# Chunks of 512 tokens in place of 384 in a fused linear-attention and feed-forward kernel

## The chip, the core and the metric

The kernel runs on one core of one Trainium2 chip. A core has five engines with queues of their own: TensorE (PE in the profile, its weight loads PEld), VectorE (DVE), ScalarE (ACT), GpSimd (POOL) and SyncE (SP), which here issues all DMAs. The metric is device time in microseconds, the median of three runs. TensorE reads operands from the on-chip SBUF and writes sums into eight PSUM banks of 128 partitions x 512 float32.

## The reference

```python
q, k, v: (8, 8, 576, 64) float32      # batch, heads, tokens, head width
kv  = einsum('bhsd,bhse->bhde', k, v)
out = einsum('bhsd,bhde->bhse', q, kv)
rms = sqrt(mean(out * out, axis=-1) + 1e-6)
x   = (out / rms * g_norm), heads side by side: (4608 tokens, 512)
h   = x @ w_in          # (512, 2048), float64 in memory
g   = h * cos(h)
y   = g @ w_out         # (2048, 512), float64 in memory -> (4608, 512)
```

## The kernel before

**Tiling.** The 4608 tokens are cut into twelve chunks of `CH = 384`, d_ff into sixteen tiles of 128. A *step* is one tile j of d_ff for one chunk. Its first half, `stage1_part`, forms h for 128 rows of d_ff and the chunk's tokens in one bank `ps_h`: four pairs of heads p, three products each (`w_hi x_hi`, `w_lo x_hi`, `w_hi x_lo`, for every factor is split into two float32r parts), so twelve matmuls of CH columns. Its second half, `stage2_part`, adds g times the tile of w_out into one bank `acc{t}` for each 128 tokens t of the chunk, three products of 512 columns each. There are 192 steps; the order of steps is chunk 0 with tiles 0 to 7, chunk 1 with tiles 0 to 7, chunk 0 with 8 to 15, chunk 1 with 8 to 15, and then each later chunk with all sixteen. The halves of chunks 0 and 1 go through DRAM (`part`).

**Between the halves** stands `act_part` (line 640): ki on ACT (the number of turns), r twice on DVE, a clip of r on DVE, the sine of r on ACT, `r = h * r` on DVE (the last reader of the bank), ghi on ACT and glo on DVE.

**Beside the steps.** `w_part` turns the float64 words of a weight tile into float32r parts: three operations m on DVE, two sg on ACT, a product sg on DVE or POOL, a copy on ACT and a difference (`wi<-sg`, `wo<-sg`) on DVE or POOL. All 32 weight tiles stay in SBUF. `kv_part` forms k^T v of a pair of heads, `x_part` a chunk's normalised x for one pair: a transpose, a split of q into qhi and qlo, products with kv, a square, a transpose and a sum on DVE, an exchange on ACT, the power on POOL, a transpose, a product, xhi on ACT and xlo. For chunks 0 and 1 ("front"), x uses TensorE's transposes. A later chunk's x is made beside the steps of the chunk before it.

**Order.** The generators above don't run on the chip: class `Order` simulates the engines with the durations written in the `yield "run"` lines and with tokens for the buffers, and instructions are issued in the order in which its engines start them. `Pinned` keeps that order, so each engine works through a fixed list, and an instruction that waits holds up all behind it. `due(i) = 20 + 4 i` is the time a step is planned for. The buffers that matter: three `ps_h` banks, three `acc` banks, two `ps_a` banks (kv and x); two ki, three r, three g; two whole chunks of xhi and xlo; pools of three for `m` and `sg` and two for qhi and qlo; two `ob` tiles for output. At the program's end the last output tile uses the slot of `kt` instead of `ob`.

All engine instructions that go through `Pinned` have line 190 in the profile, so groups are told apart by tile names.

Of the kernel before, what the change touches and what calls it, by code (L numbers as in the profile page):

```python
# [23 lines left out]
# 2*pi = C1 + C2; C1 has 8 significant bits, so k * C1 is exact for |k| < 2**16.  # L24
# [3 lines left out]
# The upper word of a float64, read as a float32, grows with the float64 as sign and magnitude.  # L28
# 2**-126, float32's smallest normal number, reads as 1.125 * 2**-15; this scale takes it just above 0.5.
# [20 lines left out]
class Order:  # L50
    """Puts the program's parts in an order by a simulation of the engines.

    A part of the program is a generator. It yields what it needs next: ("run", [(engine, us), ...], prio)
    for the use of one of these engines, ("wait", events) or ("take", tokens). After a "run" it issues its
    instructions, in the order in which the simulated engines start them; the lowest prio goes first.
    """
# [3 lines left out]
    def __init__(self):  # L60
        self.busy = {}
        self.pending = []
        self.seq = 0

    def spawn(self, gen, t=0.0):
        self.advance(Proc(gen, t), None)

    def advance(self, proc, value):
        while True:
            try:  # L70
                req = proc.gen.send(value)
            except StopIteration:
                return
# [55 lines left out]
            # the engine is taken by the lowest prio among the parts ready when it would start  # L129
# [10 lines left out]
def tile_kernel(  # L140
# [16 lines left out]
    CH = 384  # L157
# [5 lines left out]
    # The first chunks and batches are loaded in fewer transfers, and lean on TensorE, which waits then.  # L163
# [13 lines left out]
    ps_h = ctx.enter_context(tc.tile_pool(name="ps_h", bufs=3, space=bass.MemoryType.PSUM))  # L177
# [4 lines left out]
    class Pinned:  # L182
        """An engine whose instructions stay in the order in which they are issued."""
# [11 lines left out]
    def copiers(on_act, on_dve):  # L195
        return [("ACT", on_act, 0.0), ("DVE", on_dve, 0.3)]
# [18 lines left out]
    # products of zeros, for TensorE's clock is at its half until it has been busy for a while  # L215
# [28 lines left out]

    def due(i):
        return 20.0 + 4.0 * i
# [22 lines left out]
    x_slot = [Event() for _ in range(NCH)]  # L269
# [46 lines left out]
    def kv_loads_front(b, p, tags):  # L316
        """The loads of an early pair of heads, into slots of weights that come late."""
# [22 lines left out]
    def q_loads_front(c, p, tag):  # L340
        """A chunk of pairs p and p + 1, in rows of tokens."""
# [27 lines left out]
    def kv_part(b, p, prio):  # L369
        yield "wait", [kv_in[b, p]] + ([q_used[c, p] for c in chunks_of(b - 2)] if b > 1 else [])  # L370
        yield "take", t_psa, prio
        _, end = yield "run", [("PE", 0.95 if b >= FRONT else 1.1)], prio if b < FRONT else -1.0
# [14 lines left out]
        else:  # L387
            e, end = yield "run", copiers(0.21, 0.27), prio
# [6 lines left out]
        yield "run", [("ACT", 0.21)], prio  # L395
# [6 lines left out]
        _, end = yield "run", [("DVE", 0.27)], prio  # L402
# [9 lines left out]
    def kv_split_part(b, p, prio):  # L412
        """The parts of an early kv, for a chunk that isn't."""
        yield "wait", [kv_done[b, p]]
        yield "run", [("ACT", 0.18)], prio
# [8 lines left out]
    def x_tiles(c):  # L424
        yield "take", t_x
        _, _ = yield "run", [("NONE", 0.0)], -1.0
        xs[c] = (
            xpool.tile([P, NP, CH], F32R, name="xhi"),
            xpool.tile([P, NP, CH], F32R, name="xlo"),
        )  # L430
        sched.fire(x_slot[c], sched.busy["NONE"])
# [6 lines left out]
    def x_part(c, p, prio):  # L438
        yield "wait", [q_in[c, p], x_slot[c]]
        front = c < FRONT  # L440
        yield "take", t_qhl, prio
        if front:
            bank = t_psa if c else t_h
            yield "take", bank, prio
            _, _ = yield "run", [("PE", 0.4)], prio
# [6 lines left out]
        else:  # L452
            yield "take", t_qT
            _, end = yield "run", [("DVE", 0.47)], prio
# [3 lines left out]
        if front:  # L458
            e, end = yield "run", copiers(0.41, 0.47), prio
            qT = at.tile([P, CH], F32, name="qhi")  # L460
            copy(e, qT, ps_t[:, 0:CH])
            sched.give(bank, end)
        else:
            yield "run", [("ACT", 0.41)], prio
            qhi = at.tile([P, CH], F32R, name="qhi")
            qlo = at.tile([P, CH], F32R, name="qlo")
# [6 lines left out]
        bank = t_acc[p] if c == 0 and p < NTT else t_psa  # L473
        yield "take", bank, prio
        _, end = yield "run", [("PE", 0.5 if front else 0.5 if len(parts) == 1 else 0.7)], prio if front else -1.0
# [12 lines left out]
        sched.give(t_qhl, end)  # L488
        yield "take", t_s1, prio
        yield "run", [("ACT", 0.37)], prio  # L490
        sq = at.tile([P, CH], F32, name="s1", bufs=4)
        act.activation(out=sq, in_=ps[:, 0:CH], func=AF.Square, scale=0.125)
        if front:
            t_xn = t_r if c == 0 and p < NTT else t_s1
            yield "take", t_xn, prio
            _, end = yield "run", [("ACT", 0.46)], prio
            x = ew.tile([P, CH], F32, name="r") if t_xn is t_r else at.tile([P, CH], F32, name="s1", bufs=4)
            act.activation(out=x, in_=ps[:, 0:CH], func=AF.Copy, scale=gcol)
            _, end = yield "run", [("PE", 0.6)], prio
            sums = ps[:, CH:CH + 2 * NTT]  # L500
# [3 lines left out]
            yield "run", [("DVE", 0.13)], prio  # L504
            ms = small.tile([P, 2 * NTT], F32, name="ms")
            dve.tensor_scalar(out=ms, in0=sums, scalar1=EPS, scalar2=None, op0=ALU.add)
            yield "run", [("POOL", 1.2)], prio
            rinv = small.tile([P, 2 * NTT], F32, name="rinv")
            pool.tensor_tensor(out=rinv, in0=ms, in1=mhalf[:, 0:2 * NTT], op=ALU.pow)
            yield "run", [("ACT", 0.41)], prio  # L510
# [3 lines left out]
            _, end = yield "run", [("PE", 0.4)], prio  # L514
# [4 lines left out]
            _, end = yield "run", [("DVE", 0.47)], prio  # L519
            dve.tensor_tensor(out=x, in0=x, in1=ps[:, 0:CH], op=ALU.mult)  # L520
            sched.give(bank, end)
        else:
            t_xn = t_s1
            yield "take", t_s2
            yield "run", [("DVE", 0.47)], prio
            sqT = at.tile([P, TB, 32], F32, name="s2", bufs=1)
            dve.transpose(out=sqT.rearrange("p a b -> p (a b)"), in_=sq)
            _, end = yield "run", [("DVE", 0.47)], prio
# [3 lines left out]
            sched.give(t_s2, end)  # L532
            yield "run", [("ACT", 0.41)], prio
# [3 lines left out]
            yield "run", [("DVE", 0.09)], prio  # L537
            ms = small.tile([P, TB], F32, name="ms")
            dve.scalar_tensor_tensor(out=ms, in0=part, scalar=EPS, in1=swp, op0=ALU.add, op1=ALU.add)
            yield "run", [("POOL", 2.28)], prio  # L540
# [20 lines left out]
    def w_part(key, prio):  # L561
# [40 lines left out]
        sched.give(t_wst, end)  # L602
        sched.fire(w_done[key], end)

# [1 line left out]
    g_done = [Event() for _ in steps]  # L606
    g_tiles = {}

# [207 lines left out]
```

## Time and profile before

| what | us |
|---|---|
| runs: median (lowest to highest) | 937.34 (936.47 to 938.5) |
| profiled execution: span from first to last instruction (its only time given) | 933.4 |
| PE, DVE, ACT, POOL busy in it | 898.7, 722.4, 487.0, 221.2 |
| first-half matmuls, 128x384 | 2304 |
| second-half matmuls, 128x512 | 1728 |
| DMA of the whole run (not a time) | 58.59 MB |

PE's matmuls overlap one another: a matmul of 384 columns shows as 340 ns, though the next one starts earlier. The distance of starts, not the duration, says what a matmul costs. An engine that waits inside an instruction, as DVE does for a resource, shows as busy.

### The profile page before, as it was taken

What the parts mean: (1) busy time and instruction counts of PE and PEld (TensorE: products, weight loads), DVE (VectorE), ACT (ScalarE), POOL (GpSimd) and SP (SyncE); (2) the same over time, 40 slices, a digit from 0 to 9 for tenths busy, and PEclk for the clock granted to TensorE, in tenths of its full rate; (3) what the DMA queues carried; (4) which work ended last, traced back from release to release, by engine and by line L of the source; (5) the groups of instructions that cost most, each with busy time, mean ns of one, the idle gap of its engine ahead of it and who ended that gap; (6) DMA issues with size and microseconds to landing.
All of it is one profiled execution on the core that took longest, in us unless ns stands there. A gap on an engine that the chain in (4) does not pass through costs nothing.

```text
span 933.4 us, 14111 instructions
## 1 busy us (share of the span) xinstructions
PE 898.7 (96%) x5008; PEld 798.7 (86%) x5008; DVE 722.4 (77%) x1442; ACT 487.0 (52%) x1094; POOL 221.2 (24%) x148
## 2 busy tenths in 40 slices
PE   8797878999999999999999999999999999999998
PEld 6685666889889998888889999889889999999997
DVE  3999999799777777777776876786886886886664
ACT  5876666455445445455445545454553653653443
POOL 3676655122120220121120220210210220220000
PEclk7899999999999999999999999999999999999999
DMA  9997001153211102121220111220310110100000
GB/s 253 261 314 233 35 0 57 18 161 99 68 42 43 18 9 69 43 60 47 58 67 25 27 18 30 72 69 9 94 18 1 51 18 1 52 1 1 35 1 34
DMA packets 112246, 58.59 MB, mean 63 GB/s; under 512 B 80432, under 2 KB 103984, under 8 KB 112176
## 3 DMA queue, kind: packets, MB, share of 16 engines
q1 hardware_dynamic: 112176, 57.70, 22.9%
q8 instruction: 39, 0.64, 0.3%
q14 instruction: 31, 0.25, 0.1%
HBM read 46.66 MB, written 11.01 MB: 62 GB/s over the span
## 4 chain that ended last, share of the span: by engine, by line
PE 83%; DVE 10%; DMA 3%; issue 1%; SPq 1%; ACT 0%; DVEq 0%
PE acc L190 39%; PE ps_h L190 39%; PE ps_a L190 5%; DVE m L190 4%; DVE r L190 3%; DVE glo L190 2%; DMA wo<-in_moe_w_out_dram 2%; DMA wi<-in_moe_w_in_dram 1%; SPq L364 1%; DMA wo<-in_v_dram 1%; SPq L321 1%; DVE xlo L190 0%; DVE sg L190 0%; DVE s L190 0%; SPq L348 0%
## 5 line engine op out<-in xcount | busy, mean ns | idle before, releaser
L190 PE MATMUL ps_h<-xhi,wi 128*128 128x384 f32 x1536 | 398.2, 340 | 8.8 <-DVE r L190 7.7
L190 PE MATMUL acc<-wo,ghi 128*128 128x512 f32 x1152 | 363.4, 397 | 1.0 <-ACT ghi L190 0.7
L190 PEld LDWEIGHTS ps_h<-xhi,wi 128*128 128x128 f32 x1536 | 282.5, 190 | 26.3 <-DVE r L190 10.2
L190 PE MATMUL ps_h<-xlo,wi 128*128 128x384 f32 x768 | 259.8, 338 | 0.0
L190 PEld LDWEIGHTS acc<-wo,ghi 128*128 128x128 f32 x1152 | 212.2, 189 | 37.7 <-ACT ghi L190 1.6
L190 PE MATMUL acc<-wo,glo 128*128 128x512 f32 x576 | 229.6, 399 | 11.2 <-DVE glo L190 11.1
L190 POOL TENSOR_TENSOR rinv<-ms,mhalf 128x12 f32<-128x12 f32 (+1 forms) x48 | 105.4, 2197 | 443.3 <-DVE ms L190 296.0
L190 ACT ACTIVATE r<-r,half_pi 128x384 f32<-128x384 f32 x192 | 117.9, 615 | 144.4 <-DVE r L190 143.2
L190 DVE TENSOR_TENSOR glo<-r,ghi 128x384 fp32r<-128x384 f32 x192 | 116.6, 608 | 44.0 <-ACT ghi L190 38.6
L190 DVE SCALAR_TENSOR_TENSOR r<-ki,ps_h 128x384 f32<-128x384 int32 x192 | 104.9, 547 | 59.1 <-ACT ki L190 57.7
L190 PEld LDWEIGHTS ps_h<-xlo,wi 128*128 128x128 f32 x768 | 145.1, 189 | 0.0
L190 DVE TENSOR_TENSOR r<-ps_h,r 128x384 f32<-128x384 f32 x192 | 106.1, 553 | 50.2 <-ACT r L190 49.5
L190 PEld LDWEIGHTS acc<-wo,glo 128*128 128x128 f32 x576 | 108.6, 189 | 40.0 <-DVE glo L190 16.5
L190 ACT ACTIVATE ki<-ps_h 128x384 int32<-128x384 f32 x192 | 94.0, 490 | 93.1 <-PE ps_h L190 92.1
L190 ACT CAST ghi<-r 128x384 fp32r<-128x384 f32 x192 | 98.1, 512 | 76.6 <-DVE r L190 75.6
L190 DVE SCALAR_TENSOR_TENSOR r<-ki,r 128x384 f32<-128x384 int32 x192 | 121.0, 631 | 3.1
L190 DVE TENSOR_SCALAR r<-r 128x384 f32<-128x384 f32 x192 | 75.1, 392 | 3.8
L190 POOL TENSOR_TENSOR sg<-m,sg 128x512 f32<-128x512 f32 x28 | 38.7, 1383 | 38.6 <-DVE m L190 24.1
L190 ACT CAST xhi<-s 128x384 fp32r<-128x384 f32 x45 | 23.1, 513 | 47.1 <-DVE s L190 47.0
L190 POOL TENSOR_TENSOR qlo<-qT,qhi 128x384 fp32r<-128x384 f32 x18 | 20.3, 1125 | 93.4 <-ACT qhi L190 72.5
L190 ACT COPY swp<-part 32x12 f32<-32x12 f32 x160 | 31.8, 199 | 11.4 <-DVE part L190 9.2
L190 ACT ACTIVATE s<-ps_a 128x384 f32<-128x384 f32 x45 | 21.9, 486 | 14.8 <-PE ps_a L190 14.6
(104 smaller groups left out, 639.0 us busy)
## 6 DMA issues: line engine op xcount, KB each, us to landing
out_dram<-ob SPq DMA_DIRECT2D x35, 256.0 KB, 2.1
wi<-in_moe_w_in_dram SPq DMA_DIRECT2D x16, 512.0 KB, 8.4
wo<-in_moe_w_out_dram SPq DMA_DIRECT2D x16, 512.0 KB, 9.8
kt<-in_k_dram SPq DMA_DIRECT2D x24, 256.0 KB, 2.8
vt<-in_v_dram SPq DMA_DIRECT2D x24, 256.0 KB, 3.1
qb<-in_q_dram SPq DMA_DIRECT2D x112, 48.0 KB, 2.1
qb<-in_q_dram SPq DMA_DIRECT2D x96, 24.0 KB, 1.8
part<-ob SPq DMA_DIRECT2D x6, 256.0 KB, 2.1
```

The source lines that it names most:

```text
L190: return lambda *a, **kw: tc.keep_in_program_order(f(*a, **kw))
L321: nc.sync.dma_start(out=t, in_=src[b, 2 * p:2 * p + 2].rearrange("h (p i) d -> p h i d", p=SF))
L364: nc.sync.dma_start(out=t, in_=src)
```

## The change

The chunk becomes 512 tokens: nine chunks, 144 steps, twelve matmuls of 512 columns in a step's first half and four times three of 512 columns in the second. The fourth `acc` bank is taken from `ps_h`, which keeps two. Room in SBUF comes from sharing: xhi and xlo are single pairs now, six slots of each, so that four hold the current chunk and two the next (pairs 2 and 3 of chunk 0 lie in the slots of `kt` and `vt`, so the first later loads of k and v wait for chunk 0's last step); qhi and qlo use the slots `m` and `sg` of the weights, three in all (`t_two`); ki has one slot; the square's transpose shares the slot of qT, and `s1` has three slots. The planner's durations come from formulas (`dve_us`, `act_us`), a step is planned for 5.4 us, and kv of a batch is made in the window of the first chunk that needs it, no longer a chunk earlier. The two `ob` slots stay as they are. The diff without comments and plain renamings:

```diff
-    CH = 384
+    CH = 512
...
-    xpool = ctx.enter_context(tc.tile_pool(name="xpool", bufs=2))
-    wst = ctx.enter_context(tc.tile_pool(name="wst", bufs=3))
+    xpool = ctx.enter_context(tc.tile_pool(name="xpool", bufs=6))
...
-    at = ctx.enter_context(tc.tile_pool(name="at", bufs=2))
+    at = ctx.enter_context(tc.tile_pool(name="at", bufs=3))
...
-    ps_h = ctx.enter_context(tc.tile_pool(name="ps_h", bufs=3, space=bass.MemoryType.PSUM))
+    ps_h = ctx.enter_context(tc.tile_pool(name="ps_h", bufs=2, space=bass.MemoryType.PSUM))
...
+    def dve_us(f=CH, rate=1):
+        return 0.15 + f / (960 * rate)
+
+    def act_us(f=CH):
+        return 0.18 + f / 1200
...
-        return [("DVE", 0.067 + f / 960, bias), ("POOL", 0.15 + f / 480, 0.0)]
+        return [("DVE", dve_us(f), bias), ("POOL", 0.2 + f / 410, 0.0)]
...
+    STEP = 5.4
     def due(i):
-        return 20.0 + 4.0 * i
+        return 20.0 + STEP * i
...
-    t_kv, t_q, t_qT, t_qhl = Tokens(2), Tokens(2), Tokens(1), Tokens(2)
-    t_s1, t_s2, t_psa = Tokens(4), Tokens(1), Tokens(2)
-    t_x, t_wst, t_h, t_ki, t_r, t_g, t_osb = Tokens(2), Tokens(3), Tokens(3), Tokens(2), Tokens(3), Tokens(3), Tokens(2)
+    t_kv, t_q, t_qT, t_two = Tokens(2), Tokens(2), Tokens(1), Tokens(3)
+    t_s1, t_psa = Tokens(3), Tokens(2)
+    t_x, t_h, t_ki, t_r, t_g, t_osb = Tokens(6), Tokens(2), Tokens(1), Tokens(3), Tokens(3), Tokens(2)
...
+    def x_tokens(c, p):
+        return t_kv if c == 0 and p >= 2 else t_x
...
-        yield "run", [("ACT", 0.41)], prio
-        xhi, xlo = xs[c]
-        act.copy(out=xhi[:, p, :], in_=x)
-        e, end = yield "run", either(CH), prio
+        t_slot = x_tokens(c, p)
+        yield "take", t_slot, prio
+        yield "run", [("ACT", act_us())], prio if front else due(begin[c]) - 2 * STEP
+        if t_slot is t_kv:
+            xhi, xlo = (
+                kvp.tile([P, 2, SI, D], F32R, name=n).rearrange("p h i d -> p (h i d)") for n in ("kt", "vt"))
+        else:
+            xhi, xlo = (xpool.tile([P, CH], F32R, name=n) for n in ("xhi", "xlo"))
+        act.copy(out=xhi, in_=x)
+        e, end = yield "run", either(CH), prio if front else due(begin[c]) - 2 * STEP
...
-        ki = ew.tile([P, CH], I32, name="ki", bufs=2)
+        ki = ew.tile([P, CH], I32, name="ki", bufs=1)
...
-        first, n = window(chunks_of(b)[0] - 1)
+        first, n = window(chunks_of(b)[0])
         for p in range(NP):
-            i = first + 2 + p * (n - 3) // NP
-            load(2.1, due(i) - 6.0, [kv_in[b, p]], kv_loads(b, p), take=t_kv)
+            i = first + p * (n - 4) // NP
+            load(2.1, due(i) - 6.0, [kv_in[b, p]], kv_loads(b, p),
+                 wait=[x_done[0, 2], x_done[0, 3]], take=t_kv)
```

**Where the lists change, first place: PE in the middle of the program.** Before, at the end of a chunk: the second half of a step (tile 14, three accumulators) stands between two whole first halves, and each first half (eight rows, twelve matmuls) has its bank.

```order
L190 MATMUL ps_h_6922<-xhi_5434,wi15_1649 128x384 x2
L190 MATMUL ps_h_6922<-xlo_5435,wi15_1649 128x384
L190 MATMUL acc0_6281<-wo14_1684,ghi_6926 128x512 x2
L190 MATMUL acc0_6281<-wo14_1684,glo_6927 128x512
L190 MATMUL acc1_6299<-wo14_1684,ghi_6926 128x512 x2
L190 MATMUL acc1_6299<-wo14_1684,glo_6927 128x512
L190 MATMUL acc2_6306<-wo14_1684,ghi_6926 128x512 x2
L190 MATMUL acc2_6306<-wo14_1684,glo_6927 128x512
L190 MATMUL ps_h_6955<-xhi_6152,wi0_239 128x384 x2
```

With the change, in the middle of a chunk, a second half (tile 11, four accumulators) stands inside the first half of tile 13; the next row begins the first half of tile 14.

```order
L193 MATMUL ps_h_5897<-xhi_5105,wi13_1445 128x512 x2
L193 MATMUL ps_h_5897<-xlo_5106,wi13_1445 128x512
L193 MATMUL acc0_5281<-wo11_1483,ghi_5894 128x512 x2
L193 MATMUL acc0_5281<-wo11_1483,glo_5895 128x512
L193 MATMUL acc1_5292<-wo11_1483,ghi_5894 128x512 x2
L193 MATMUL acc1_5292<-wo11_1483,glo_5895 128x512
L193 MATMUL acc2_5310<-wo11_1483,ghi_5894 128x512 x2
L193 MATMUL acc2_5310<-wo11_1483,glo_5895 128x512
L193 MATMUL acc3_5316<-wo11_1483,ghi_5894 128x512 x2
L193 MATMUL acc3_5316<-wo11_1483,glo_5895 128x512
L193 MATMUL ps_h_5897<-xhi_5113,wi13_1445 128x512 x2
L193 MATMUL ps_h_5897<-xlo_5114,wi13_1445 128x512
```

What moved: the first half of tile 14 reuses the bank of tile 12, and between the two PE has only tile 13's first half and one second half.

**Second place: DVE while the weights are converted.** Names m are weights, r and glo the chain of `act_part`, ms and xlo early x. Before:

```order
L190 TENSOR_TENSOR glo_1198<-r_1118,ghi_1197 128x384
L190 TENSOR_SCALAR r_1192<-r_1192 128x384
L190 TENSOR_SCALAR m_1148<-m_1148 128x512
L190 TENSOR_SCALAR m_1228<-wi11_851 128x512
L190 SCALAR_TENSOR_TENSOR r_1231<-ki_1218,ps_h_1173 128x384
L190 TENSOR_TENSOR r_1192<-ps_h_1093,r_1192 128x384
L190 SCALAR_TENSOR_TENSOR r_1231<-ki_1218,r_1231 128x384
L190 SCALAR_TENSOR_TENSOR m_1228<-wi11_851,m_1228 128x512
L190 TENSOR_TENSOR glo_1255<-r_1192,ghi_1254 128x384
```

With the change, around the same weight tile:

```order
L193 TENSOR_TENSOR glo_1227<-r_1165,ghi_1226 128x512
L193 TENSOR_SCALAR r_1218<-r_1218 128x512
L193 TENSOR_SCALAR m_1254<-wi11_706 128x512
L193 SCALAR_TENSOR_TENSOR m_1254<-wi11_706,m_1254 128x512
L193 TENSOR_TENSOR r_1218<-ps_h_1149,r_1218 128x512
L193 SCALAR_TENSOR_TENSOR r_1277<-ki_1269,ps_h_1222 128x512
L193 TENSOR_SCALAR m_1286<-wo9_720 128x512
L193 TENSOR_TENSOR glo_1280<-r_1218,ghi_1279 128x512
```

What moved: little; from one glo to the next stand the same four operations of the chain and about three of the weights, the chain's now 512 wide.

**Third place: the end of ACT's list,** the copies of the last accumulators to output. Before:

```order
L190 ACTIVATE r_9673<-r_9673,half_pi_93 128x384
L190 CAST ghi_9694<-r_9673 128x384
L190 COPY ob_9710<-acc0_9212 128x512
L190 COPY ob_9716<-acc1_9219 128x512
L190 COPY kt_9718<-acc2_9225 128x512
```

With the change:

```order
L193 CAST ghi_8243<-r_8219 128x512
L193 COPY ob_8253<-acc0_7713 128x512
L193 COPY ob_8258<-acc1_7719 128x512
L193 COPY kt_8265<-acc3_7729 128x512
L193 COPY ob_8268<-acc2_7724 128x512
```

What moved: a fourth copy stands at the end, and its tile `ob` is one of the two that acc0 and acc1 went out through.

More of the change, by code (lines that the diff above doesn't have):

```diff
@@ L387, in kv_part @@
         else:
-            e, end = yield "run", copiers(0.21, 0.27), prio
+            e, end = yield "run", [("ACT", 0.41, 0.0), ("DVE", 0.45, 0.3)], prio
             for j in range(2):
@@ L531, in x_part @@
             sched.give(t_s1, end)
-            sched.give(t_s2, end)
-            yield "run", [("ACT", 0.41)], prio
+            sched.give(t_qT, end)
+            yield "run", [("ACT", 0.8)], prio
             swp = small.tile([P, TB], F32, name="swp")
@@ L601, in w_part @@
         w_split[key] = w
-        sched.give(t_wst, end)
+        sched.give(t_two, end)
         sched.fire(w_done[key], end)
@@ L628, in stage1_part @@
             w = w_split["wi", j]
-            xhi, xlo = xs[c]
+            xhi, xlo = xs[c, p]
             cols = slice(p * P, (p + 1) * P)
@@ L753, in tile_kernel @@
                 sched.spawn(g_part())
-    for c in range(NCH):
-        sched.spawn(x_tiles(c))
     for c in range(FRONT):
@@ L786, in tile_kernel @@
     sched.run()
+    assert not sched.live, sorted({x.gen.__name__ for x in sched.live})
 _INS = ['q', 'k', 'v', 'g_norm', 'moe_w_in', 'moe_w_out']
```

149 lines of the change are left out of this document (73 added, 76 removed).

## The prediction

> **What bounds the kernel now.** I read the page first: the busy shares, the slices over time, and the chain that ended last.
>
> ```profile
> span 933.4 us, 14111 instructions
> PE 898.7 (96%) x5008; PEld 798.7 (86%) x5008; DVE 722.4 (77%) x1442; ACT 487.0 (52%) x1094; POOL 221.2 (24%) x148
> PE   8797878999999999999999999999999999999998
> DVE  3999999799777777777776876786886886886664
> PE 83%; DVE 10%; DMA 3%; issue 1%; SPq 1%; ACT 0%; DVEq 0%
> ```
>
> The slices (23 us each) show two regimes: for seven slices DVE stands at 9 and PE at 7 or 8, after that PE never falls below 9. The chain, in order of time, says where one gives way to the other, and the busy times by stretch say how completely.
>
> ```profile
> 162.24 1.60 DVE glo L190
> 163.89 1.87 PE acc L190 x7
> 165.76 2.62 PE ps_h L190 x15
> ...
> 0.00:40.00 40.00, 32.65 (x280) 27.05 (x280) 23.43 (x44) 26.22 (x57) 20.85 (x27) 0.87 1.08 257
> 40.00:165.76 125.76, 102.05 (x499) 84.18 (x500) 124.22 (x193) 82.69 (x165) 79.56 (x57) 0.93 0.42 132
> 165.76:929.80 764.04, 764.04 (x4230) 687.49 (x4229) 574.75 (x1207) 377.48 (x872) 120.77 (x65) 1.00 0.16 40
> 929.80:933.40 3.60, 0.01 (x1) 0.00 (x0) 0.00 (x0) 0.58 (x1) 0.00 (x0) 1.00 0.57 219
> ```
>
> Columns after the length are PE, PEld, DVE, ACT and POOL busy. From 40 to 165.76 us DVE is busy 124.22 of 125.76 us and sets the pace (it converts the weights there); from 165.76 to 929.80 PE is busy without a gap at clock 1.00; 3.60 us of output follow. So the change is worth what it does to DVE's list before 165.76, to PE's list after it, and what new holes it tears in PE.
>
> **PE's list.** The main question is whether a matmul of 512 columns costs less per column than one of 384. Starts of runs in PE's timeline:
>
> ```profile
> 842.02 0.63 PE L190 MATMUL acc<-wo,ghi 128*128 128x512 f32 x2
> ...
> 844.10 0.51 PE L190 MATMUL ps_h<-xhi,wi 128*128 128x384 f32 x2
> ...
> 848.29 0.63 PE L190 MATMUL acc<-wo,ghi 128*128 128x512 f32 x2
> ```
>
> Nine 512-wide ones from 842.02 to 844.10 are 231.1 ns each, 0.4514 ns a column; 24 of 384 from 844.10 to 848.29 are 174.6 ns each, 0.4547 a column. Columns are the same in sum (192 x 12 x 384 = 144 x 12 x 512, and 1728 sums of 512 in both), so width by itself gives 884,736 x 0.0033 ns = 2.9 us and no more. What moves time is how much of PE's list is done while DVE is the bound:
>
> ```profile
> L190 PE MATMUL ps_h<-xhi,wi 128*128 128x384 f32 x173 | 49.4, 366 | 8.8 <-DVE r L190 7.7 <-POOL wi L190 1.0
> L190 PE MATMUL acc<-wo,ghi 128*128 128x512 f32 x120 | 40.3, 418 | 1.0 <-ACT ghi L190 0.7 <-ACT ob L190 0.2
> L190 PE MATMUL ps_h<-xlo,wi 128*128 128x384 f32 x86 | 30.0, 349 | 0.0
> L190 PE MATMUL acc<-wo,glo 128*128 128x512 f32 x60 | 26.0, 433 | 11.2 <-DVE glo L190 11.1
> ```
>
> These are PE's groups from 0 to 165.76: 259 / 12 = 21.6 first halves of steps and 180 / 9 = 20.0 second halves. Left over are 170.4 x 12 x 174.6 ns = 357.0 and 172 x 9 x 231.1 = 357.7, together 714.7 us; the other 49.3 of the 764.04 are kv and x. With 512, the same 21.6 and 20.0 steps carry a third more tokens, and left over are 122.4 x 12 x 231.1 = 339.5 and 124 x 12 x 231.1 = 343.9, together 683.4. **PE's term: -31.3.** kv has the same products; x has 43,008 columns times pairs and parts left instead of 46,080, 1.4 us, of which more narrow pieces take some: **-1**.
>
> **DVE's list up to there.** The thirty-two weights are the same work. Up to the twentieth glo, DVE's list holds 96 weight operations before and after, 100 of the element-wise chain in both, and in all 233 against 237 instructions (the extra ones small copies, against two products that move to POOL: about nothing). So the chain's operations are counted once per step, and grow. What 512 costs over 384:
>
> ```profile
> L190 DVE TENSOR_TENSOR r<-ps_h,r 128x384 f32<-128x384 f32 x192 | 106.1, 553 | 50.2 <-ACT r L190 49.5
> L190 DVE TENSOR_TENSOR ob<-ob,acc 128x512 f32<-128x512 f32 x6 | 4.0, 674 | 0.0
> ...
> 110.55 0.35 DVE L190 TENSOR_SCALAR r<-r 128x384 f32<-128x384 f32 x1
> 111.16 0.41 DVE L190 TENSOR_SCALAR m<-m 128x512 int32<-128x512 int32 x1
> ```
>
> +121 ns for an operation on tensors, +60 for the clip: 4 x 121 + 60 = 0.54 us a step, 10.9 for 20 steps, and 16 such operations in the early x (a product and an xlo for eight pairs) 1.9: **+13 is the lower end.** But many early durations are longer than that:
>
> ```profile
> 113.85 1.65 DVE L190 TENSOR_TENSOR glo<-r,ghi 128x384 fp32r<-128x384 f32 x1
> 117.13 0.54 DVE L190 SCALAR_TENSOR_TENSOR r<-ki,ps_h 128x384 f32<-128x384 int32 x1
> 118.57 0.55 DVE L190 SCALAR_TENSOR_TENSOR r<-ki,r 128x384 f32<-128x384 int32 x1
> ...
> 113.77 1.32 POOL L190 TENSOR_TENSOR sg<-m,sg 128x512 f32<-128x512 f32 x1 [0.45 <-DVE m L190]
> 116.61 1.75 POOL L190 TENSOR_TENSOR wo<-sg,wo 128x512 fp32r<-128x512 f32 x1
> ```
>
> glo begins 0.08 us after a POOL product and lasts 1.65 instead of 0.55, to 0.41 us after POOL's end; r<-ki,ps_h, which reads PSUM, runs in 0.54 beside POOL. If all durations grew by a third, waits included, the chain's five operations up to 180 us bound it:
>
> ```profile
> L190 DVE TENSOR_TENSOR glo<-r,ghi 128x384 fp32r<-128x384 f32 x23 | 22.1, 963 | 2.3 <-ACT ghi L190 2.3
> L190 DVE SCALAR_TENSOR_TENSOR r<-ki,r 128x384 f32<-128x384 int32 x24 | 20.7, 866 | 0.1
> L190 DVE TENSOR_TENSOR r<-ps_h,r 128x384 f32<-128x384 f32 x24 | 13.1, 548 | 2.6 <-ACT r L190 2.6
> L190 DVE SCALAR_TENSOR_TENSOR r<-ki,ps_h 128x384 f32<-128x384 int32 x24 | 12.9, 541 | 0.0
> L190 DVE TENSOR_SCALAR r<-r 128x384 f32<-128x384 f32 x24 | 10.2, 429 | 0.2
> ```
>
> The five means give 3.35 us a step, and 20 x 1.1 + 2 is **+24, the upper end.** I take **+16**, near the lower: the wait ends with POOL's instruction, which is a weight's and keeps its size. The Trainium skill, "SBUF — State Buffer", section "SBUF: two separate sides", says that DVE and GpSimd hold a shared pair of ports by an exclusive lock for a whole instruction; these rows agree, and by that rule alone the term would be +13, by growth in proportion +24.
>
> **Waits that the change makes.** ps_h has two banks instead of three. A bank is held from the first product of a step until `r = h * r` has read it. One such chain of before, ACT and DVE:
>
> ```profile
> 841.84 0.34 PE L190 MATMUL ps_h<-xlo,wi 128*128 128x384 f32 x1
> 842.28 0.49 ACT L190 ACTIVATE ki<-ps_h 128x384 int32<-128x384 f32 x1 [1.21 <-PE ps_h L190]
> 842.80 0.56 DVE L190 SCALAR_TENSOR_TENSOR r<-ki,ps_h 128x384 f32<-128x384 int32 x1 [1.14 <-ACT ki L190]
> 843.77 0.52 DVE L190 SCALAR_TENSOR_TENSOR r<-ki,r 128x384 f32<-128x384 int32 x1
> 844.73 0.35 DVE L190 TENSOR_SCALAR r<-r 128x384 f32<-128x384 f32 x1
> 845.27 0.62 ACT L190 ACTIVATE r<-r,half_pi 128x384 f32<-128x384 f32 x1
> 845.91 0.56 DVE L190 TENSOR_TENSOR r<-ps_h,r 128x384 f32<-128x384 f32 x1
> ```
>
> From PE's end (842.18) to the release (846.47) are 4.29 us, with three operations of x between. At 512 the six operations gain 3 x 0.12 + 0.06 on DVE and about 2 x 0.1 on ACT, the three between 0.36: 5.3 us. In the new order PE has, between the last product of a step and the first of the step after next, one first half and one second half: 24 x 0.2311 = 5.55 us. Before, with three banks, it was 8.2 us or more in all but some twenty steps, and 6.2 in most of those. So a typical chain just fits; with one more x operation of 0.68 ahead PE waits 0.4. Queued behind PE's waiting matmul are the second halves, which free accumulators and g. Bounds: 0, if the order keeps x out of the tight steps, and 15 us, if one step in four of the 123 left waits 0.5. I take **+5**, nearer the lower, as DVE has more room per step than before (5.55 us of PE for 3.1 of chain, against 4.18 for 2.5, by the rows just shown and a glo of 0.55).
>
> **The two ends.** Ahead of the first step, pairs 2 and 3 of chunk 0 pass a third more columns through DMA, PE and ACT, while DVE partly idles (23.43 of 40 us): 0 to 2, **+1**. At the end four tiles go out through two `ob` slots and one `kt`: the copy of acc2 waits for the first store and stands behind kt's on ACT. In the 3.60 us of before, one copy took 0.58 and its store the rest; a store that begins some 1.2 us later: **+1.2** (0.5 to 1.5).
>
> Sum: -31.3 - 1 + 16 + 5 + 1 + 1.2 = -9.1; the span 933.4 becomes 924.3. The median of the runs, 937.34, is 3.9 above the span, so I predict **928 us**. All lower ends give -31.3 - 1 + 13 + 0 + 0 + 0.5 = -18.8 (918.5), all upper ones -32.3 + 24 + 15 + 2 + 1.5 = +10.2 (947.5). The likeliest case alone spans 920 to 935.
>
> **Rivals.** (1) *The bank decides, slower.* If the chain is late by 0.4 us in every step, PE loses 123 x 0.4 = 49 us in place of the 5: 972. It turns slower than before from (9.1 + 5) / 123 = 0.11 us a step on; around 0.2 it is 948. For it: 5.3 against 5.55 leaves a quarter microsecond. Against: it is PE's own waiting that lets DVE catch up. (2) *The early stretch gives it all back.* Weights and early x now share three `m`/`sg` slots, and ki has one: if DVE, full today, idles for 5 us and the waits grow in proportion (+24), the sum is -9.1 + 5 + 8 = +4, 941; with one of the two, about no change. (3) *A matmul has a cost of its own*, so 576 fewer pay. At a cost of c ns each 576 c is saved; the two spacings above allow 0.0033 x 512 = 1.7 ns by this trace. The Trainium skill, "TensorE: Matmul & The Clock Gate", section "Back-to-back issue gap", gives a sustained 81 ns at 128 columns and 131 at 512, hence an estimate of 114 at 384: by that rule a third more width costs 1.15 times, and 1728 x 174.6 x 1.15 against 2304 x 174.6 saves 55 us, 877 in all. The trace does not agree: 174.6 to 231.1 is 1.32 times.
>
> **How the numbers follow.** Forecast 0.62; rival 1 0.21; rival 2 0.15, of which 0.06 on the slower side; rival 3 0.02. Runs of this kernel tell no change from a change within about 0.2%, 1.9 us. Faster: 0.62 + 0.02 + 0.02 of rival 2 = 0.66; within: 0.07 of rival 2 and 0.01 of 1 = 0.08; slower: 0.26 (0.20 and 0.06). The range reaches from all lower ends into rival 1: 918 to 946.
>
> **What would show it.** Right: 512-wide first halves about 231 ns apart; DVE full until some 180 us, PE from then on without gaps; r and glo unblocked at about 0.67. Wrong: PE idle, with DVE r named as releaser of ps_h, in many steps after 200 us (rival 1); PE first dense after 195 us, or DVE idle between 40 and 180 (rival 2).

## The result and the profile after

Twelve runs of each kernel on the same chip: before 937.12 us median (935.21 to 939.79), with chunks of 512 tokens 937.49 us (935.32 to 941.15). The ratio is 1.0005, its 95% interval 0.9991 to 1.0019: no difference can be told. The profiled executions, whose span is one sample each, stand at 933.4 and 935.9 us.

The page of the changed kernel, the lines that answer to those shown of before: span, busy times, slices of 23 us, the chain that ended last.

```profile
span 935.9 us, 12295 instructions
PE 892.8 (95%) x4464; PEld 722.7 (77%) x4464; DVE 679.0 (73%) x1122; ACT 449.6 (48%) x860; POOL 214.1 (23%) x128
PE   8688887899999999999999999999999999999998
DVE  2987999967868776777677767776776677765664
PE 61%; DVE 5%; POOL 2%; issue 1%; ACT 1%; DMA 0%; POOLq 0%; SPq 0%; ACTq 0%; DVEq 0%
```

The early regime of the kernel before (DVE at 9, PE at 7 or 8) now has a dent: DVE's third and fourth digits are 8 and 7. The same ledger as in the prediction needs the moment at which the same work is done. PE's groups of the changed kernel up to 201.2 us, by shape (pairs 2 and 3 of chunk 0 have the names kt and vt):

```profile
L193 PE MATMUL acc<-wo,ghi 128*128 128x512 f32 x160 | 52.0, 406 | 1.7 <-DVE wo L193 1.7
L193 PE MATMUL ps_h<-xhi,wi 128*128 128x512 f32 x120 | 43.8, 448 | 15.6 <-DVE r L193 15.4 <-POOL wi L193 0.3
L193 PE MATMUL acc<-wo,glo 128*128 128x512 f32 x80 | 32.3, 404 | 0.6 <-DVE glo L193 0.6
L193 PE MATMUL ps_h<-xlo,wi 128*128 128x512 f32 x60 | 25.8, 431 | 0.0
L193 PE MATMUL ps_h<-kt,wi 128*128 128x512 f32 x53 | 17.2, 405 | 0.6 <-ACT kt L193 0.6
L193 PE MATMUL ps_h<-vt,wi 128*128 128x512 f32 x26 | 10.3, 395 | 0.8 <-DVE vt L193 0.8
```

(120 + 60 + 53 + 26) / 12 = 21.6 first halves and (160 + 80) / 12 = 20.0 second halves: the state that the kernel before had at 165.76 us. Busy times by stretch (PE, PEld, DVE, ACT, POOL, then the granted clock), of the changed kernel and, in the second fence, of the kernel before:

```profile
20.00:201.20 181.20, 151.87 (x747) 118.64 (x746) 158.73 (x231) 113.36 (x203) 102.44 (x69) 0.92 0.44 125
201.20:931.60 730.40, 725.28 (x3595) 592.20 (x3593) 516.58 (x882) 327.13 (x640) 104.67 (x43) 1.00 0.17 43
931.60:935.90 4.30, 0.07 (x1) 0.00 (x0) 0.00 (x0) 1.17 (x2) 0.00 (x0) 0.87 0.53 200
```

```profile
20.00:165.76 145.76, 118.44 (x642) 98.41 (x639) 142.45 (x224) 98.71 (x198) 92.15 (x66) 0.93 0.52 151
```

From these rows and the 764.04 and 3.60 us of the prediction:

| term | forecast | measured |
|---|---|---|
| DVE's list up to the equal state, busy from 20 us on | +16 | 158.73 - 142.45 = +16.3 |
| DVE idle in that stretch, with the start | +1 | 22.47 - 3.31 = +19.2 |
| PE busy from there to the end of its list | -32.3 | 725.28 - 764.04 = -38.8 |
| PE idle there (two banks) | +5 | 730.40 - 725.28 = +5.1 |
| output after PE's end | +1.2 | 4.30 - 3.60 = +0.7 |
| sum | -9.1 | +2.5 |

The expected gain on PE came, and 6.5 us more than expected. It was given back early, by idle time of DVE. Where DVE idles, in its own timeline of the changed kernel:

```profile
58.07 1.51 DVE L193 TENSOR_SCALAR m<-m 128x512 int32<-128x512 int32 x1
...
64.40 0.68 DVE L193 COPY m<-ps_a 128x512 f32<-128x512 f32 x1
...
69.51 0.69 DVE L193 TENSOR_TENSOR glo<-r,ghi 128x512 fp32r<-128x512 f32 x1 [0.69 <-ACT ghi L193]
71.60 0.69 DVE L193 COPY m<-ps_a 128x512 f32<-128x512 f32 x1 [1.40 <-PE ps_a L193]
...
74.40 0.42 DVE L193 TENSOR_SCALAR m<-wi 128x512 int32<-128x512 uint32 x1
75.08 0.68 DVE L193 SCALAR_TENSOR_TENSOR m<-wi,m 128x512 int32<-128x512 int32 x1
```

Between 59.58 and 74.40 us there is no operation of a weight in DVE's list, though 22 of the 32 weights are still to come. What stands there is `m<-ps_a`: chunk 1's transposed q, which now lies in a slot of the weights and holds it until the product with kv of its pair has read it. (The order takes the slot even before q's transpose; of the copies to m, the one of 64.40 and one of ACT at 66.69 are read by products that start at 69.92 and 73.54.) Without weights in between, the next operation of DVE's list is often one of a step's chain that waits for ACT. DVE's own waits for ACT's ki and sine, up to 200 us in the changed kernel (summed time, times, longest):

```profile
DVE r L193 <- ACT ki L193: 6.7, 5, 2.8
DVE r L193 <- ACT r L193: 4.1, 5, 1.6
```

In the kernel before, up to 170 us, the second kind has 1.0 us and the first does not appear:

```profile
DVE r L190 <- ACT r L190: 1.0, 2, 0.7
```

And PE stands, up to 205 us, for these:

```profile
PE ps_h L193 <- DVE r L193: 15.4, 8, 3.8
PE ps_a L193 <- DMA wo<-in_v_dram: 6.8, 2, 3.6
```

The second row is another suspect: chunk 1's v, whose load has a later due time since a step is planned longer. The first row names the banks of h.

### The profile page after: what moved, and what is told of

Its sections match the earlier page's. It is cut to its first block, busy times and chain, and to the rows that moved or that the text cites. A ratio compares the mean times of both kernels' runs of the same rounds, so it can differ in the third digit from the quotient of the medians.

```text
span 935.9 us, 12295 instructions
## 1 busy us (share of the span) xinstructions
PE 892.8 (95%) x4464; PEld 722.7 (77%) x4464; DVE 679.0 (73%) x1122; ACT 449.6 (48%) x860; POOL 214.1 (23%) x128
## 4 chain that ended last, share of the span: by engine, by line
PE 61%; DVE 5%; POOL 2%; issue 1%; ACT 1%; DMA 0%; POOLq 0%; SPq 0%; ACTq 0%; DVEq 0%
PE acc L193 29%; PE ps_h L193 29%; PE ps_a L193 4%; DVE r L193 3%; POOL rinv L193 2%; DVE s L193 1%; DVE qT L193 0%; DVE glo L193 0%; DVE part L193 0%; ACT ki L193 0%; POOLq L827 0%; DVE xlo L193 0%; DMA vtt<-in_v_dram 0%; DMA out_dram<-ob 0%; ACT s L193 0%
## 5 line engine op out<-in xcount | busy, mean ns | idle before, releaser
L193 PE MATMUL ps_h<-xhi,wi 128*128 128x512 f32 x1088 | 346.3, 400 | 19.9 <-DVE r L193 19.5
L193 PE MATMUL ps_h<-xlo,wi 128*128 128x512 f32 x544 | 214.8, 395 | 0.0
L193 ACT ACTIVATE r<-r,half_pi 128x512 f32<-128x512 f32 x144 | 104.2, 723 | 146.5 <-DVE r L193 146.1
L193 POOL TENSOR_TENSOR rinv<-ms,mhalf 128x16 f32<-128x16 f32 (+1 forms) x36 | 98.6, 2740 | 324.2 <-DVE ms L193 301.6
L193 DVE SCALAR_TENSOR_TENSOR r<-ki,ps_h 128x512 f32<-128x512 int32 x144 | 98.3, 683 | 69.9 <-ACT ki L193 69.1
L193 DVE TENSOR_TENSOR r<-ps_h,r 128x512 f32<-128x512 f32 x144 | 99.2, 689 | 66.9 <-ACT r L193 66.1
L193 ACT ACTIVATE ki<-ps_h 128x512 int32<-128x512 f32 x144 | 85.9, 597 | 115.9 <-PE ps_h L193 96.6
L193 DVE TENSOR_TENSOR glo<-r,ghi 128x512 fp32r<-128x512 f32 x144 | 104.0, 722 | 38.1 <-ACT ghi L193 37.1
L193 ACT CAST ghi<-r 128x512 fp32r<-128x512 f32 x144 | 89.0, 618 | 67.2 <-DVE r L193 67.1
L193 DVE SCALAR_TENSOR_TENSOR r<-ki,r 128x512 f32<-128x512 int32 x144 | 113.6, 789 | 1.9
L193 DVE STREAM_TRANSPOSE qT<-s 128x512 f32<-128x512 f32 x28 | 19.8, 708 | 12.8 <-ACT s L193 12.8
```

The costliest lines, as they stand in the source:

```text
L193: return lambda *a, **kw: tc.keep_in_program_order(f(*a, **kw))
```

## The experiments

All kernels but one are the changed one with the edit shown; "before" is the kernel with 384, run beside them (medians 936.3 to 936.7 us). The medians are of two to eight runs, those of e6 and e8 of one. The table has, for each but e6, the moment of the equal state (the same counts as above; in e9 and e10 nearly so) and DVE's busy and idle time from 20 us to it, by the same view.

| kernel | median us | equal state at | DVE busy | DVE idle |
|---|---|---|---|---|
| before | 937.12 | 165.76 | 142.45 | 3.3 |
| the change | 937.49 | 201.2 | 158.73 | 22.5 |
| e1: own slots for chunk 1's q | 929.45 | 193.5 | 159.02 | 14.5 |
| e2: early loads | 940.53 | 204.8 | 157.78 | 27.0 |
| e3: e1 and e2 | 931.61 | 196.6 | 160.33 | 16.3 |
| e8: two ki early | 935.74 (one run) | 199.1 | 159.97 | 19.1 |
| e5: chain as one | 930.99 | 198.3 | 160.00 | 18.3 |
| e7: e1 and e5 | 922.82 | 190.4 | 157.29 | 13.1 |
| e11: e7, chunk 0's q too | 921.87 | 189.1 | 159.88 | 9.2 |
| e10: three banks for h | 933.62 | 197.7 | 156.97 | 20.7 |
| e9: before, with shared slots | 942.30 | 172.1 | 142.01 | 10.1 |

DVE's busy time is the same within 2.2% in all of 512, and what moves the equal state is mostly its idle time.

**e1: own slots.**

```diff
-        yield "take", t_two, prio
+        t_mine = t_osb if c == 1 else t_two
+        yield "take", t_mine, prio
...
-            qT = at.tile([P, CH], F32, name="m")
+            qT = osb.tile([P, CH], F32, name="ob") if c == 1 else at.tile([P, CH], F32, name="m")
...
-        sched.give(t_two, end)
+        sched.give(t_mine, end)
```

> The edit: chunk 1's transposed q lies in the two output tiles ob, which are idle until about 127 us, and no longer in the m slots that the weights use. Theory A (the shared slots empty DVE's list of weights): the hole between the tenth and the eleventh m of the weights (59.6 to 76.2 us after the change) shrinks below 9 us, the point at which 20.8 steps are done moves from 201 to about 189 us, and the span from 935.9 to about 925. Theory B (late loads of chunk 1's k and v): PE still waits 3.6 and 3.2 us for them near 45 and 49 us, the point stays within 3 us of 201, the span within 3 us of 936. Theory C (DVE's list and its waits for POOL simply grew by a third): no change either, and DVE stays as empty between 60 and 80 us.

The median fell to 929.45 (ratio to before 0.990, 0.9865 to 0.9936), the equal state came 7.7 us earlier, and from there to the end nothing else changed. DVE between 60 and 80 us, first the change, then e1 (the third column after the length):

```profile
60.00:80.00 20.00, 19.53 (x99) 15.66 (x98) 13.06 (x21) 10.41 (x18) 7.75 (x5) 1.00 0.92 240
```

```profile
60.00:80.00 20.00, 20.00 (x139) 16.07 (x138) 19.58 (x32) 14.85 (x29) 13.89 (x10) 1.00 0.86 223
```

So theory A has the mechanism, at less than its size: it foresaw 12 us and got 7.7. Theories B and C foresaw nothing.

**e2: early loads, and e3: both.**

```diff
-            t = due(begin[c]) - 28 + 3 * p if c else -100.0 + p
+            t = 24.0 + 3 * p if c else -100.0 + p
```

> The edit: the loads of chunk 1's q, k and v get back the due times that they had before the change (24, 27, 30 and 33 us; with the longer step they had moved to 35 to 44), so that fewer weights go ahead of them on SyncE's queue. Theory B: PE's waits of 3.6 and 3.2 us for in_v near 45 and 49 us vanish, the third first half ends near 40 us and not at 58.2, and the point at which 20.8 steps are done moves from 201 to about 191 us, the span to about 926. Theory A: PE's two waits vanish, but the hole in the weights' conversion stays, and the span stays within 3 us of 936. Theory C: within 3 us as well.

> The edits of the runs e1 and e2 together: chunk 1's transposed q in the two ob slots, and its loads at their earlier due times. Theory A alone (slots matter, loads don't, even when the slots are free): the same as e1, 929.5 within 2 us, 20.8 steps done near 193. Theory A+B (with free slots the early loads can be used): x of chunk 1 comes earlier, DVE fills between 40 and 60 us and is idle 10 us less than in e1 up to that point; some 5 to 10 us faster than e1, 920 to 924. If the loads only push weights back, as e2's +2.5 to +4 us says: 932 to 933.

e2 was slower than before (1.0037, 1.0017 to 1.0058), its span 2.4 us over the change's. PE's longest waits for in_v fell from 3.6 and 3.2 us to 2.1 and less, and behind them stood the next wait, in PE's timeline of e2:

```profile
51.94 1.22 PE L193 MATMUL ps_h<-xhi,wi 128*128 128x512 f32 x2 [7.01 <-DVE r L193]
```

The third first half has to wait for the bank of the first one anyway, and that is released by DVE; in the change the same matmul starts at 50.95 us. So the third first half ended at 59.7 us against 58.2, and the weights came later. Also with free slots (e3), where PE's waits for in_v are 1.1 us in all, the early loads bring nothing: 931.61 us against e1's 929.45, a difference near the spread of the runs. Theory B falls: the 6.8 us of PE waiting for v were hidden.

**e9: the same sharing in the kernel before.** Edited is the kernel with chunks of 384; three slots as in the change, and the weights take them by the priority of their part, as there.

```diff
-        yield "take", t_qhl, prio
+        yield "take", t_wst, prio
...
-            qT = at.tile([P, CH], F32, name="qhi")
+            qT = wst.tile([P, DM], F32, name="m")[:, 0:CH]
...
-            qhi = at.tile([P, CH], F32R, name="qhi")
-            qlo = at.tile([P, CH], F32R, name="qlo")
+            qhi = wst.tile([P, DM], F32R, name="m")[:, 0:CH]
+            qlo = wst.tile([P, DM], F32R, name="sg")[:, 0:CH]
...
-        sched.give(t_qhl, end)
+        sched.give(t_wst, end)
...
-        yield "take", t_wst
+        yield "take", t_wst, prio
```

> The edit, in the kernel before (chunks of 384): q's parts take the slots m and sg of the weights, three in all, as in the change, in place of two of their own; nothing else. Theory A (sharing the slots by itself takes weights out of DVE's list): a hole of 5 us or more in the weights' conversion between 45 and 80 us, DVE's idle time from 20 to about 170 us grows from 3.3 us by 5 to 10, and the time from 937 to 942 to 947. Rival (the hole needs the change's late loads and longer early x as well): DVE stays full and the time stays within 2 us of 937.

942.30 us, 1.0052 times before (1.0029 to 1.0075). DVE up to the near-equal state (22.0 first halves, 19.8 second ones):

```profile
20.00:172.10 152.10, 124.68 (x649) 102.65 (x646) 142.01 (x226) 100.22 (x203) 94.01 (x65) 0.90 0.50 145
```

Busy as before (142.01 against 142.45), idle 10.1 against 3.3: sharing by itself makes the loss, from the other side, with the old loads and the old chunk. The single hole of 5 us that theory A named did not appear; the idle time is spread from 20 to 80 us (16.20, 18.45 and 17.47 us busy in stretches of 20, against 18.23, 20.00 and 19.45).

**e8: a second ki slot early.**

```diff
-        yield "take", t_ki
+        t_mine = t_osb if i < 12 else t_ki
+        yield "take", t_mine, prio
...
-        ki = ew.tile([P, CH], I32, name="ki", bufs=1)
+        ki = osb.tile([P, CH], I32, name="ob") if i < 12 else ew.tile([P, CH], I32, name="ki", bufs=1)
...
-        sched.give(t_ki, end)
+        sched.give(t_mine, end)
```

> The edit: the first twelve steps keep ki in the two ob slots, so that it has two slots there, as before the change, and one only from the thirteenth step on. Theory A (only the weights' slots empty DVE's list): the hole between the tenth and the eleventh m stays, 20.8 steps done within 3 us of 201, span within 3 us of 936. Rival (the single ki slot is a part of DVE's idle time, as the prediction's second rival had it): DVE's idle time up to that point falls from 22 us by 5 or more, and the span by as much.

Idle time fell by 3.3 us up to the equal state, which came 2.1 us earlier; span 934.0 against 935.9. All of that is within theory A's bounds, and the rival's 5 us were not reached. The single ki slot has a small share at most, and a single run with 2 us can't tell it from none.

**e5: the chain planned as one.**

```diff
-        yield "run", [("DVE", dve_us())], prio
+        _, end = yield "run", [("DVE", 2 * dve_us() + dve_us(CH, 2))], prio
         r = ew.tile([P, CH], F32, name="r")
         dve.scalar_tensor_tensor(out=r, in0=ki, scalar=-C1, in1=h, op0=ALU.mult, op1=ALU.add)
-        _, end = yield "run", [("DVE", dve_us())], prio
         dve.scalar_tensor_tensor(out=r, in0=ki, scalar=-C2, in1=r, op0=ALU.mult, op1=ALU.add)
         sched.give(t_ki, end)
-        yield "run", [("DVE", dve_us(CH, 2))], prio
```

> The edit: the three operations on DVE between ki and the sine are planned as one, so that no operation of x or of a weight can stand between them. Theory D (the holes of PE after 201 us, about 11 us in all, come from operations of x that stand between these three and hold the bank): the time from the last product of a first half to the release of its bank falls from a median of 5.17 us to about 4.5, the idle time of PE after 201 us falls from 11 to under 4 us, and the span by about 7 us. Rival D2 (the holes come from other operations ahead of the chain or from ACT's part of it): latency and holes stay, span within 3 us. Rival D3 (x is pushed late by it): new waits of PE for x at the starts of chunks, span longer by some us.

930.99 us (0.992, 0.988 to 0.996). One chain on DVE, of the change and then of e5, from the first r to the product that releases the bank:

```profile
433.16 0.68 DVE L193 SCALAR_TENSOR_TENSOR r<-ki,ps_h 128x512 f32<-128x512 int32 x1
433.75 0.70 DVE L193 STREAM_TRANSPOSE qT<-s 128x512 f32<-128x512 f32 x1
434.38 0.65 DVE L193 SCALAR_TENSOR_TENSOR r<-ki,r 128x512 f32<-128x512 int32 x1
434.95 0.67 DVE L193 TENSOR_REDUCE part<-qT 128x16 f32<-128x512 f32 x1
435.55 0.41 DVE L193 TENSOR_SCALAR r<-r 128x512 f32<-128x512 f32 x1
436.53 0.17 DVE L193 SCALAR_TENSOR_TENSOR ms<-part,swp 128x16 f32<-128x16 f32 x1 [0.57 <-ACT swp L193]
437.28 0.69 DVE L193 TENSOR_TENSOR r<-ps_h,r 128x512 f32<-128x512 f32 x1 [0.57 <-ACT r L193]
```

```profile
427.73 0.68 DVE L193 SCALAR_TENSOR_TENSOR r<-ki,ps_h 128x512 f32<-128x512 int32 x1
428.44 0.69 DVE L193 SCALAR_TENSOR_TENSOR r<-ki,r 128x512 f32<-128x512 int32 x1
429.17 0.43 DVE L193 TENSOR_SCALAR r<-r 128x512 f32<-128x512 f32 x1
429.51 0.17 DVE L193 SCALAR_TENSOR_TENSOR ms<-part,swp 128x16 f32<-128x16 f32 x1
430.39 0.69 DVE L193 TENSOR_TENSOR r<-ps_h,r 128x512 f32<-128x512 f32 x1 [0.71 <-ACT r L193]
```

4.81 us become 3.35. Over steps 20 to 139, worked out from each step's own rows, the median time from the end of a first half to the release fell from 5.17 to 4.49 us, as theory D said. But of the 6.7 us of span 2.9 were gained before the equal state, where the same grouping lets DVE idle 4.2 us less, and only 3.8 after it; that the sum comes near theory D's 7 is luck. The expectation's "11 us of holes" was read too high: it held every start of a matmul that came later than 226.7 ns after the one before, and the windows from 205 to 900 us have 5.1 us of PE idle. Of these e5 removed 1.6 (a new hole of 2.0 at 877 us included). Most of the other 2.2 is in delays too short to count as idle: after the equal state the products of first halves start 230.8 ns apart on average, against 232.0 in the change (1469 of them, 1.8 us).

**e10: three banks for h, one for kv and x.**

```diff
-    ps_h = ctx.enter_context(tc.tile_pool(name="ps_h", bufs=2, space=bass.MemoryType.PSUM))
-    ps_a = ctx.enter_context(tc.tile_pool(name="ps_a", bufs=2, space=bass.MemoryType.PSUM))
+    ps_h = ctx.enter_context(tc.tile_pool(name="ps_h", bufs=3, space=bass.MemoryType.PSUM))
+    ps_a = ctx.enter_context(tc.tile_pool(name="ps_a", bufs=1, space=bass.MemoryType.PSUM))
```

with `t_h` and `t_psa` of three and one tokens.

> The edit: three banks for h, as before the change, and one bank for kv and x in place of two; everything else as in the change. The prediction's two-bank term (+5 us after the stretch where DVE is the bound): PE's idle time from 205 to 900 us, 5.1 us with two banks, falls under 1.5 us if nothing else makes it wait, the span by some 4 us. Rival (the bank for kv and x is needed twice: a product of x that waits for the one bank holds up PE's list): new idle time with ps_a as what was waited for, as long or longer than the 5 us, and the early x of chunk 1 later; span the same or up to 10 us more. If the early stretch too suffered from the two banks (in e1 and e2 PE stands 7 us for a bank near 45 us), the point at which 20.8 steps are done moves from 201 to 196 or earlier.

933.62 us (0.9964, 0.9943 to 0.9985); span 4.1 us shorter than the change's. PE by stretch, first the change, then e10:

```profile
205.00:360.00 155.00, 151.83 (x800) 123.34 (x799) 116.87 (x203) 68.74 (x144) 32.26 (x14) 0.99 0.29 75
360.00:900.00 540.00, 538.06 (x2642) 439.84 (x2641) 380.36 (x649) 245.66 (x476) 72.41 (x29) 1.00 0.14 36
```

```profile
205.00:360.00 155.00, 148.70 (x782) 121.14 (x781) 116.82 (x202) 67.96 (x142) 29.00 (x12) 0.98 0.29 75
360.00:900.00 540.00, 540.00 (x2663) 445.09 (x2662) 384.54 (x651) 246.67 (x478) 73.24 (x31) 1.00 0.14 36
```

After 360 us the third bank closes all holes (1.94 to 0.00 us), so those were the bank's. Before 360 they grew (3.17 to 6.30): one of 3.3 us still for the release of h, one of 2.6 at a ps_a for which no releaser shows; why is open. So from 205 us on PE idles 1.2 us more than in the change, and the shorter span comes from ahead of it; the last case of the expectation, with 196 us or earlier, was near this. At 197.7 us 22.0 first halves and 19.6 second ones are done, together as many as in the change at 201.2:

```profile
20.00:197.70 177.70, 152.62 (x740) 115.90 (x740) 156.97 (x225) 113.96 (x209) 97.16 (x67) 0.92 0.44 128
```

PE's 15.4 us of early waits for ps_h are 4.1 here, while its waits for ps_a behind ACT grew from 0.8 to 4.9. So the two banks cost time in the early stretch too, some 3.5 us.

**e6: halves of 256 columns.**

```diff
-        for p in range(NP):
+        for f, p in [(f, p) for f in range(2) for p in range(NP)]:
+            half = slice(f * 256, f * 256 + 256)
...
-                    out=h, lhsT=w[:, s, cols], rhs=x,
+                    out=h[:, half], lhsT=w[:, s, cols], rhs=x[:, half],
```

> The edit: each product of a first half is issued as two of 256 columns (first all of one half of the tokens, then the other), 1728 matmuls more with the same columns in sum. Theory E (in a pure run a matmul costs 0.4164 ns a column and 13.4 ns of its own, as 173.3 ns at 384 and 226.6 at 512 say): 120 ns from start to start at 256 columns, a first half takes 2.88 us against 2.72, and with a slower start after each change of width (some 5 ns for the first nine products) the span grows by about 25 us. Rival E2 (0.45 ns a column and at most 1.7 ns of its own, the reading of the prediction): 117 ns or less, and the span grows by at most 3 us. Rival E3 (the weight load of each matmul, 162 ns long on average in the profile, becomes the limit): 162 ns, first halves of 3.9 us, and some 140 us more.

The span grew by 20.6 us, to 956.5. Starts in PE's timeline, of e6 first and then of the change:

```profile
833.01 0.40 PE L193 MATMUL ps_h<-xhi,wi 128*128 128x256 f32 x2
...
835.17 0.63 PE L193 MATMUL acc<-wo,ghi 128*128 128x512 f32 x2
...
837.92 0.40 PE L193 MATMUL ps_h<-xhi,wi 128*128 128x256 f32 x2
```

```profile
841.03 0.62 PE L193 MATMUL acc<-wo,ghi 128*128 128x512 f32 x2
...
843.75 0.61 PE L193 MATMUL ps_h<-xhi,wi 128*128 128x512 f32 x2
```

Eighteen matmuls of 256 from 833.01 to 835.17 are 120.0 ns each, exactly theory E's number. Twelve of 512 that follow them take 2.75 us (229.2 ns each); twelve of 512 that follow others of 512 take 2.72 (226.7). Theory E foresaw about 25; the growth follows: a first half takes 24 x 120.0 = 2.88 us instead of 2.72, times the 122.4 that are left after the equal state 19.6 us. E2 (at most 3 us) and E3 (162 ns) fall.

**e7 and e11: what beats both kernels.** e7 is e1 and e5 together; e11 gives chunk 0's transposed q an ob slot too (`c < FRONT` in place of `c == 1`).

> The edits of e1 and e5 together: chunk 1's transposed q in the ob slots, and the three operations of the chain on DVE planned as one. If the two gains (7.7 us early, 6.7 us of which about 3 are early and 4 late) are independent: 937.5 - 7.7 - 6.7 = 923, faster than both kernels. If e5's early part came from the same idle time of DVE that e1 takes away: about 926. If the planner's new order makes a hole elsewhere: 928 or more.

> The edits of e7, and chunk 0's transposed q in the ob slots as well, so that none of the early q lies in the slots of the weights. Theory A (slots shared with q take weights out of DVE's list, also ahead of the first step, where DVE is idle for 5 us of 20 to 40): one to four us faster than e7, 919 to 922. Rival (ahead of the first step DVE waits for loads, not for slots): within 1.5 us of e7's 922.8.

e7: 922.82 us, 0.9855 (0.9825 to 0.9886); the sum of the two gains is that of the expectation's first case (923). e11: 921.87 us, 0.9853 (0.9831 to 0.9875). e11 is 1.3 us shorter by span than e7 and 0.95 by median, less than can be told apart, with idle time of DVE down from 13.1 to 9.2 us. The page of e11:

```profile
span 918.4 us, 12263 instructions
PE   8799898999999999999999999999999999999998
DVE  2899999959888767887678767776777688765654
```

## Why the prediction was wrong

Forecast 928 us, faster with 0.66; measured no change, which had 0.08. By its own steps:

**DVE's list: size right, its fullness wrong.** "I take +16" met 16.3 us of busy time. It lies nearer to the +13 that was worked out by the rule of the Trainium skill's "SBUF — State Buffer", section "SBUF: two separate sides", than to growth in proportion (+24). The step that failed is that this sum of durations was let stand for the time of the list: DVE was taken to stay as full as before (124.22 of 125.76 us), and its idle time was put at +1, for the start alone. It measured +19.2. The prediction counted the operations up to the twentieth glo and did not ask whether the next entry of the list is ready. The entries that moved into the gap, chunk 1's q in slots of the weights, wait for kv, and the weights behind them were not issued. e1 gives back 8.0 of the 19.2 us of idle time and 7.7 us of span, and e9 makes 6.8 us of idle time out of the sharing alone. The grouped chain gives 4.2, chunk 0's q 3.9 beside e7, a second slot of ki 3.3 in its one run. These overlap (e7's 9.4 is less than 8.0 + 4.2), and e11 still idles 5.9 us more than before. The cause of that rest is not shown. The two banks are one candidate: up to 205 us PE waits 13.3 us for ps_h in e11 too, and e10's third bank moved the equal state by 3.5 us. No run joins the two.

**Rival 2 was the case.** It named the shared slots and the single ki, and gave "5 us" of idle time and a chance of 0.15. The part of the slots is shown; its size alone was 8, and the whole idle time 19. Its other half, waits that grow in proportion, did not come. The signs that it set ("PE first dense after 195 us, or DVE idle between 40 and 180") are both in the profile. That "about no change" came out, as it had it for one half alone, is luck: almost four times its idle time met a PE term that was 6.5 us better.

**PE's term: 6.5 us too small.** "Width by itself gives ... 2.9 us and no more" rested on 231.1 and 174.6 ns, both read just behind a change of width, and 231.1 was used for both kernels. Worked out from the distances of starts after the equal state, idle time taken out:

| matmuls | forecast, before to after | measured, before to after |
|---|---|---|
| first halves | 357.0 to 339.5 = -17.5 | 360.3 to 340.9 = -19.4 |
| second halves | 357.7 to 343.9 = -13.8 | 359.1 to 340.4 = -18.7 |
| kv and x | -1 | 44.3 to 43.6 = -0.7 |

So most of the miss is in the second halves. Their products have 512 columns in both kernels, but start 232.1 ns apart on average before, behind first halves of 384, and 228.9 in the change, where first halves have 512 too. The first halves' products start 176.2 and 232.0 ns apart on average. How a change of width matters is seen in the kernel before, where the prediction's run from 844.10 to 848.29 has this row in its middle:

```profile
846.21 0.51 PE L190 MATMUL ps_h<-xhi,wi 128*128 128x384 f32 x2
```

The first twelve matmuls of that run take 175.8 ns each, the next twelve 173.3. With 226.7 at 512 that is 53.4 ns for 128 columns, 0.417 a column, and 13 ns that each matmul costs beside its columns; e6 confirmed the line at 256. So rival 3 (0.02) was partly true. The prediction allowed it 1.7 ns, but its own spacings leave 174.6 - 384 x 56.5 / 128 = 5.1 ns, and 576 x 5.1 ns are the 2.9 us that it had already counted. The Trainium skill, "TensorE: Matmul & The Clock Gate", section "Back-to-back issue gap", has a formula for a single matmul of N / 2.4 + 2.5 ns: the slope agrees, the constant here is 13. The sustained 131 ns at 512 of the same section, from which the rival had its 55 us, is not seen: 226.7.

**Two banks: +5, measured 5.1.** PE's waits from 205 to 900 us bear out the term, by name:

```profile
PE ps_h L193 <- DVE r L193: 4.2, 8, 1.9
```

e10 shows only the 1.9 us after 360 to be the bank's; for the earlier ones the cause is not shown, and with bounds of 0 to 15 the close hit is in part luck. That two banks would cost in the early stretch too, some 3.5 us by e10, was not in the prediction. **The ends:** +0.7 against +1.2. Rival 1 (a wait in every step) did not come.

**The median above the span** was taken as 3.9 us; of the changed kernel it is 1.6. In every run with both on record, the time is 1.7 to 1.8 us above its own span. So the profiled 933.4 us of before belong to a run of about 935.2, 1.9 under the median, and that is most of what parts the ledger's +2.5 of spans from the +0.4 of medians.

With some of the early holes taken out the change is faster than the kernel before: by 1.0% with e1 alone, by 1.5% in e11. Part of the latter is e5's grouping, which was not tried in the kernel before.

## What to carry to other kernels

Where a fixed list is the bound, its sum of durations is only the lower bound of its time: for each buffer that two kinds of work come to share, ask which of them holds it while it waits for something else, and what of the other kind then drops out of the list. A spare buffer that is idle at that moment (here the output tiles) can give a part of it back. And take the cost of an instruction from a place like the one that it will have after the change: next to a change of width if one will stand there, in a long run of its own kind if not.

## What the runs showed of the hardware

Streams of these matmuls, each with a weight load of its own, start 120.0, 173.3 and 226.7 ns apart at 256, 384 and 512 columns, at granted clock 1.00 and once a run is long enough: about 13.4 ns and 0.4164 ns a column. Behind a change of width the next nine to twelve are slower by 2.5 ns (512 after 256) to 4.4 ns (512 after 384: 231.1 against 226.7). The cause of the latter was not looked into.
